# A fixed slot and engine for every operation of an attention and gated-projection kernel, in place of a greedy list order

## The chip, the core and the metric

One core of a Trainium2 chip runs the whole program. The metric is the device time of one execution in microseconds (us). The kernel before took 273.78 us, the median of 3 runs (273.67 to 274.02).

## What is computed

Four batches, 8 heads, 768 positions, head size 64, all in 32-bit floats. Attention sees a window of 96 past positions and the first 8 positions, with a linear bias per head; its output x goes through a 5-tap causal convolution that makes a gate, and through two 512 x 512 projections.

```python
scores = scale * np.matmul(q, k.transpose(0, 1, 3, 2))          # + bias, masked
a = np.exp(scores); a = a / (np.sum(a, axis=-1, keepdims=True) + 1e-09)
attn = np.matmul(a, v)                                          # x: (B, S, H * D)
gate = 1.0 / (1.0 + np.exp(-gate_pre))                          # gate_pre: 5 taps over x
return (gate * (x @ w_val) @ w_out).astype(np.float32)
```

## The kernel before, in words

The work is cut into 32 groups (`groups`: batch, half of the sequence, pair of heads), 3 steps of 128 queries each (96 steps), and 8 phases (a batch's half: 4 groups). The program is a list of 1,854 operations with names. Per group: `L` and `LV` load keys, queries and values (SP queue), `S` makes the score tiles on TensorE (PE). Per step: `AM` adds the bias and takes the row minimum (VectorE, DVE), `EX` takes the exponential (ScalarE, ACT), `RG` guards the sum (L511), `RC` inverts it (L514, DVE), `NM` multiplies the probabilities by it, once per head (L519), `PT` transposes them on PE through the identity (L530), `EV` copies the result out of PSUM. Per pair of groups `PV` multiplies with the values (L547, L553) into the PSUM tile x. From x come `XH` and `XL` (a rounded high part and the rest, for matmuls in the fp32r format), `HO` and `HI` (four columns of history, handed from half to half) and five `CV` (the taps, `gate`, L658 and L660). Per phase: `SG` (half a tanh), 16 `VM` (projection val, L706, three matmuls each), 4 `GM` (gate times val, L713), 4 `GH` and `GL` (high and low part, L720), 12 `OM` (projection o, L729, three matmuls each), 3 `OE` (evacuation, L740) and 3 `ST` (stores, L747).

The weights arrive as 64-bit floats and are decoded in the first part of the program: for each of 8 blocks `WL` (load, L404), `WA` (ACT), `W1` to `W4` (DVE), `WH` (high part), `WS` (sum on PE, L414 to L416), `WP` (its evacuation). `WARM` and `F` are matmuls on constants that fill PE's time at the start (L292); `plan.fill` puts such matmuls ahead of some transposes (L525).

Every operation has an urgency (constants such as `U_AM`, shifted per phase by `SHIFT`), a cost per engine that may run it, and what it depends on; `Plan.order` walks through time with a greedy rule: of the engine that is free first, the ready operation with the smallest urgency is taken, and an operation that several engines can run goes to the one that ends it first (with `SPARE` added). The order that comes out is each engine's instruction stream; instructions of one engine run in that order. `ring` makes an operation wait for the reader of a buffer that it will write again: the PSUM tiles of val and o share 2 banks (`moe`), the scores 2 per head, x 2.

```python
first = min(cands)
_, i, e = min(((ops[i][0], i, e) for t, i, e in cands if e == first[2] and t <= first[0] + LOOK[e]))
```

Of the kernel before, what the change touches and what calls it, by code (L numbers as in the profile page):

```python
# [16 lines left out]
WARM = 10  # L17
S_B, PT_B, X_B = 2, 2, 2
U_D1, RAW_B = -7.17, 4
FILL_UNTIL = 80.0  # L20
FILL_N, FILL_TO, U_F = 4, 1, -1.44
W_AT = (-0.71, 5.47, 7.21, 10.78, 17.96, 19.59, 23.37, 34.85)
W_PARTS = (2, 2, 2, 2, 2, 1, 1, 1)
WS_AT = (1, 4, 7, 10, 15, 19, 22, 24)
LOOK = {'vector': 0.0, 'scalar': 0.0, 'gpsimd': 0.0, 'tensor': 0.0, 'sync': 0.0}
SPARE = {'vector': 0.91, 'gpsimd': 0.02, 'scalar': -1.19}
XH_B, GATE_B, P_B, T_B, A_B, V_B, W_B, WT_B = 7, 2, 5, 8, 13, 6, 2, 1
U_XE, U_XH, U_CV, CV_STEP = -0.42, 0.63, 4.12, 0.63
U_AM, U_EX, U_RC, U_PT, U_EV, U_MOE = -0.95, -0.12, -5.71, -0.76, 4.31, 19.31
LAG = 2  # L30
JOIN = (0, 0, 0, 0, 1, 1, 1, 1, 1, 1, 1, 1, 1, 1, 1, 1)
U_L, U_LV, U_WL, U_S, U_HI, U_NM = -21.33, 0.02, -9.24, -2.77, 2.74, 0.27
U_PH = (-4.87, -0.47, -0.79, -0.74, -0.89, -0.15, -4.34, 2.72)
U_SG, U_GM, GM_STEP, U_GH, U_GL, U_O, VAL_T, O_T, U_OE = 13.64, -0.98, 0.8, -2.75, 0.05, 3.03, 5.41, 0.97, 1.65
SHIFT = {
# [49 lines left out]
class Plan:  # L85


    LAT = {'scalar': 0.2, 'vector': 0.19, 'gpsimd': 0.09, 'tensor': 0.24, 'sync': 0.05}
    DMA_LAT, DMA_RATE = 1.6, 330e3

    def __init__(self):
        self.ops, self.at, self.rings, self.then, self.fill = [], {}, {}, {}, {}

    def add(self, key, urgency, engines, fn, deps=(), nbytes=0, bank=None):

        assert key not in self.at, key
# [19 lines left out]
    def order(self, start):  # L116
        ops, at = self.ops, self.at
        n = len(ops)
        free, dma = dict(start), 0.0
        end, where = [0.0] * n, [""] * n  # L120
        left, users = [0] * n, [[] for _ in range(n)]
        deps = [sorted({at[d] for d in op[3]}) for op in ops]
        for i in range(n):
            left[i] = len(deps[i])
            for d in deps[i]:
                users[d].append(i)

        def ready(i, e):
            return max([end[d] + (0.05 if where[d] == e else self.LAT[where[d]]) for d in deps[i]], default=0.0)

        avail = [i for i in range(n) if not left[i]]
        out = []
        while avail:
            cands = []
            for i in avail:
                t = {e: max(free[e], ready(i, e)) for e in ops[i][1]}
                e = min(t, key=lambda x: t[x] + ops[i][1][x] + SPARE.get(x, 0.0))
                cands.append((t[e], i, e))
            first = min(cands)
            _, i, e = min(  # L140
                ((ops[i][0], i, e) for t, i, e in cands if e == first[2] and t <= first[0] + LOOK[e])
            )
            while i is not None:
                t = max(free[e], ready(i, e))
# [7 lines left out]
                if nbytes:  # L152
                    dma = max(dma, t + cost) + nbytes / self.DMA_RATE
                    end[i] = dma + self.DMA_LAT
# [893 lines left out]
```

## Time and profile before

| what | value |
|---|---|
| median of 3 runs | 273.78 us |
| the profiled execution: its own time | 274.04 us |
| its span, first to last instruction | 272.2 us |
| busy: PE, DVE, ACT, POOL | 260.0, 188.4, 209.4, 133.1 us |
| instructions | 8800 |
| chain that ended last, by engine | PE 76%, DVE 8%, DMA 6%, ACT 4% |

PE is TensorE (PEld its weight loads), POOL is GpSimd, SPq the queue that issues DMAs. A timeline row gives the start, the duration, the engine and line, the operation with output and inputs, and in brackets the idle time ahead of it and who ended it. Durations of neighbouring instructions of an engine overlap, so the price of one more in a dense run is the distance from start to start. A table of windows gives for each stretch the busy time of each engine.

### The profile page before, as it was taken

How to read it: one execution, taken by the hardware profiler on the slowest of the kernel's cores; microseconds unless marked ns; L12 is line 12 of the kernel's file. 1: busy time of each engine (PE TensorE's matmuls, PEld its weight loads, DVE VectorE, ACT ScalarE, POOL GpSimd, SP SyncE). 2: the span in 40 equal slices, each digit the busy share in tenths (PEclk: the TensorE clock that was granted, in tenths of full speed). 3: DMA queues.
4: the chain of work that ended last, by engine and by line, in shares of the span. 5: the costliest groups of instructions: out<-in, count | busy, mean ns of one | idle time of the engine just before them, and what ended most of it. 6: DMA issues, size and time to landing. Idle time of an engine off the chain costs nothing.

```text
span 272.2 us, 8800 instructions
## 1 busy us (share of the span) xinstructions
PE 260.0 (96%) x3125; PEld 216.7 (80%) x3127; DVE 188.4 (69%) x752; ACT 209.4 (77%) x701; POOL 133.1 (49%) x332
## 2 busy tenths in 40 slices
PE   8788999899899999999999999999999999999994
PEld 3447778677688888978898889888898889987983
DVE  4867999898939484785849493877769475494610
ACT  4899999888978788787778787987878695675322
POOL 5776666646346724364447634462447443350220
PEclk9999999999999999999999999999999999999998
DMA  5877876451645164513454153425551020002003
GB/s 169 300 256 220 318 258 236 138 164 56 209 118 191 47 192 141 158 67 95 172 169 135 56 207 119 159 69 161 166 177 51 4 79 39 2 39 81 0 5 122
DMA packets 16304, 36.37 MB, mean 134 GB/s; under 512 B 1920, under 2 KB 4480, under 8 KB 16256
## 3 DMA queue, kind: packets, MB, share of 16 engines
q1 hardware_dynamic: 16256, 35.75, 39.6%
q8 instruction: 27, 0.44, 0.7%
q14 instruction: 21, 0.17, 0.2%
HBM read 29.46 MB, written 6.29 MB: 131 GB/s over the span
## 4 chain that ended last, share of the span: by engine, by line
PE 76%; DVE 8%; DMA 6%; ACT 4%; issue 2%; SPq 2%; POOL 1%; POOLq 0%; ACTq 0%
PE o L729 25%; PE val L706 19%; PE pt L530 9%; PE s L486 9%; PE x L547 8%; DMA kq<-in_kq 6%; PE x L553 5%; DVE gate L658 4%; ACT p L504 2%; DVE xl L650 1%; DVE t L494 1%; PE wsum L414 1%; DVE g L713 1%; ACT gate L660 1%; POOL p L519 1%
## 5 line engine op out<-in xcount | busy, mean ns | idle before, releaser
L519 POOL TENSOR_SCALAR p<-p,rs 128x168 f32<-128x168 f32 (+1 forms) x186 | 79.9, 441 | 39.7 <-DVE rs L514 28.6
L504 ACT ACTIVATE p<-t,mins 128x168 f32<-128x168 f32 (+1 forms) x192 | 81.6, 427 | 7.9 <-DVE mins L494 5.8
L658 DVE SCALAR_TENSOR_TENSOR gate<-x,cwt,gate 128x384 f32<-128x384 f32 x128 | 78.3, 613 | 0.6
L494 DVE CUSTOM_DVE_ANT_0 t<-s,bias 128x168 f32<-128x168 f32 (+1 forms) x192 | 56.6, 318 | 7.6 <-PE s L486 7.5
L706 PE MATMUL val<-xh,wvh 128*128 128x384 f32 x128 | 48.1, 376 | 1.1 <-DVE g L713 1.1
L530 PE MATMUL pt<-ident,p 128*128 128x128 f32 x272 | 47.2, 278 | 1.4 <-ACT wvl L188 0.5
L188 ACT COPY a<-pt 128x384 f32<-128x384 f32 (+1 forms) x96 | 43.3, 454 | 6.6 <-PE pt L530 6.6
L511 POOL TENSOR_SCALAR sm<-sm 128x2 f32<-128x2 f32 x96 | 20.0, 208 | 54.2 <-ACT p L504 48.0
L720 POOL TENSOR_TENSOR gl<-g,gh 128x384 fp32r<-128x384 f32 x28 | 28.5, 1020 | 32.2 <-ACT gh L188 31.0
L729 PE MATMUL o<-woh,gh 128*128 128x512 f32 (+1 forms) x100 | 42.1, 421 | 1.7 <-DVE g L713 0.9
L706 PE MATMUL val<-xh,wvl 128*128 128x384 f32 x128 | 43.1, 337 | 0.0
L706 PE MATMUL val<-xl,wvh 128*128 128x384 f32 x128 | 43.1, 337 | 0.0
L530 PEld LDWEIGHTS pt<-ident,p 128*128 128x128 f32 x272 | 33.6, 140 | 10.5 <-POOL p L519 2.3
L729 PE MATMUL o<-wol,gh 128*128 128x512 f32 (+1 forms) x100 | 38.7, 387 | 0.0
L729 PE MATMUL o<-woh,gl 128*128 128x512 f32 (+1 forms) x100 | 38.6, 386 | 0.0
L504 ACT ACTIVATION_READ_ACCUMULATOR p<-t,mins 128x1 f32 x192 | 36.8, 192 | 0.0
L486 PEld LDWEIGHTS s<-kq 64*64 64x64 f32 x1088 | 30.3, 133 | 7.9 <-issue 4.4
L486 PE MATMUL s<-kq 64*64 64x104 f32 (+3 forms) x1088 | 34.3, 262 | 2.4 <-DMA kq<-in_kq 2.3
L514 DVE RECIPROCAL rs<-sm 128x2 f32<-128x2 f32 x96 | 15.5, 161 | 28.9 <-POOL sm L511 28.2
L650 DVE TENSOR_TENSOR xl<-x,xh 128x384 fp32r<-128x384 f32 x32 | 17.6, 554 | 22.0 <-ACT gate L660 12.6
L706 PEld LDWEIGHTS val<-xh,wvh 128*128 128x128 f32 x128 | 24.2, 189 | 3.7 <-DVE g L713 2.3
L188 ACT CAST xh<-x 128x384 fp32r<-128x384 f32 x32 | 15.2, 486 | 14.7 <-PE x L553 14.7
(154 smaller groups left out, 371.0 us busy)
## 6 DMA issues: line engine op xcount, KB each, us to landing
kq<-in_kq SPq DMA_DIRECT2D x16, 444.0 KB, 4.3
va<-in_va SPq DMA_DIRECT2D x16, 384.0 KB, 4.6
out<-ob SPq DMA_DIRECT2D x24, 256.0 KB, 2.1
kq<-in_kq SPq DMA_DIRECT2D x15, 392.0 KB, 3.9
va<-in_va SPq DMA_DIRECT2D x16, 320.0 KB, 3.9
w<-in_wv SPq DMA_DIRECT2D x8, 256.0 KB, 3.6
w<-in_wo SPq DMA_DIRECT2D x3, 512.0 KB, 4.4
w<-in_wo SPq DMA_DIRECT2D x2, 256.0 KB, 3.4
```

What stands on the lines that cost most here:

```text
L188: nc.scalar.copy(dst, src)
L486: nc.tensor.matmul(s[rows, u : u + w], T["rq", g][r, k * P + half * QH : k * P + (half + 1) * QH], T["rk", g][r, c : c + w], start=True, s ...
L494: nc.vector.tensor_tensor_reduce(out=t[:, :n], in0=T["s", s // HB, s % HB, j][:, :n], in1=bias[:, h, :P] if n == P else bias[:, h, P:], op ...
L504: nc.scalar.activation(T["p", s][:, j, :n], T["t", s, j][:, :n], AF.Exp, bias=mins[:, s, j : j + 1], scale=-1.0, accum_out=T["sm", s][:, j ...
L519: engine(e).tensor_scalar(out=pr, in0=pr, scalar1=rs, scalar2=1.0, op0=ALU.mult, op1=ALU.mult)
L530: nc.tensor.transpose(pt[:, i * P : (i + 1) * P], pr[:, c : c + P], ident)
L547: nc.tensor.matmul(T["x", g][rows(i), c0 : c0 + P], T["near", g][:, k, j], T["a", HB * g + k][:, j * P : (j + 1) * P], start=k == 0, stop= ...
L650: engine(e).tensor_sub(tile_of(("xl", g), [P, HT], F32R, "xl", XH_B), T["x", g][:, HIST:], T["xh", g])
L658: nc.vector.scalar_tensor_tensor(out=gt, in0=src, scalar=w, in1=gt, op0=ALU.mult, op1=ALU.add)
L706: nc.tensor.matmul(T["val", ph, m], (wvh, wvh, wvl)[r][:, m, c * P : (c + 1) * P], (T["xh", g], T["xl", g], T["xh", g])[r], start=(c == 0 ...
L720: engine(e).tensor_sub(tile_of(("gl", ph, m), [P, HT], F32R, "gl", 5), T["g", ph, m], T["gh", ph, m])
L729: nc.tensor.matmul(T[key][:, cols], (T["gh", ph, c], T["gl", ph, c], T["gh", ph, c])[r][:, rows], (woh, woh, wol)[r][:, c, cols], start=(c ...
```

## The change

`Plan.order` no longer simulates anything. Two tables replace urgencies, costs and rule: `SLOTS` gives each operation of a kind, in the order in which the kind's operations are added, a place in one list of 1,854, and `ENGINES` an engine where more than one can run it. `order` sorts by slot. `FILL` names the one transpose that still has a constant matmul ahead of it (before: 4 of them ahead of two transposes). Some dependencies are changed: the buffers `wh` and `wr` of the decoding are free again when `WS` has read them, not when `WP` has ended; `WH` waits for `W2` alone; `AM` names the bias of the head that it really uses; `F` waits for the scores alone. `PV` depends on `HI` (the history's write into x) as before. Arithmetic and shapes stay.

```diff
+SLOTS = {
+    "L": (
+        2, 5, 8, 16, 89, 132, 136, 183, 188, 275, 391, 400, 503, 506, 601, 606, 618, 655, 719, 760, 829, 853, 943,
...
+ENGINES = {
+    "BIAS": "SSSSSGSGSGGSGSSS",
...
+    "GL": "GGVVGVVGGGGGGGVVGVVVVGGGGVGGGVVG",
+    "OE": "SSSSSSSSVSSVSSVSSSVSVSVVS",
 }
+FILL = {7: 1}
...
+        kind = key[0]
+        n = self.count[kind] = self.count.get(kind, -1) + 1
+        e = NAMES[ENGINES[kind][n]] if kind in ENGINES else engines[0]
...
+    def order(self):
+        for slot, _, _, deps in self.ops:
+            assert all(self.ops[self.at[d]][0] < slot for d in deps), "an operation is listed before one that it needs"
+        return [(fn, e) for _, e, fn, _ in sorted(self.ops, key=lambda op: op[0])]
...
-        for _ in range(plan.fill.get(plan.at["PT", s], 0)):
+        for _ in range(FILL.get(s, 0)):
...
-                deps += plan.ring("wh", WT_B, key, [("WP", i), ("WH", i)])
+                deps += plan.ring("wh", WT_B, key, [("WS", i), ("WH", i)])
...
-                deps += plan.ring("wr", WT_B, key, [("WP", i)])
+                deps += plan.ring("wr", WT_B, key, [("WS", i)])
...
-        plan.add(("WH", i), u + 0.5, {ACT: 0.52, DVE: 0.335}, lambda e, i=i: w_high(e, i), [("W2", i), ("W3", i)])
+        plan.add(("WH", i), (ACT, DVE), lambda e, i=i: w_high(e, i), [("W2", i)])
...
-                         [("S", g), ("BIAS", 2 * groups[g][2] + j, int(full))] + plan.ring("t", T_B, key, [("EX", s, j)]))
+                plan.add(key, (DVE,), lambda e, s=s, j=j: add_bias(s, j),
+                         [("S", g), ("BIAS", 2 * groups[g][2] + head_at(groups[g][2], j), int(full))]
+                         + plan.ring("t", T_B, key, [("EX", s, j)]))
```

What moves between engines, counted in the two orders: to DVE go 53 of POOL's 186 `NM`, 51 of its 96 `RG` and 9 of its 28 `GL`; from ACT, DVE takes 9 first taps of `CV`, 7 `GH`, 7 `OE` (one of them a half), 6 `EV`, 5 `XH`, 7 copies of history and one `WH`; ACT takes 3 `BIAS` from POOL.

The SP queue at the start of the program issues the first DMAs (kq: keys and queries of a group, va: values, w: a weight block, craw: the taps). Before:

```order
L225 DMA counts_i<-in_counts 128x4
L266 DMA kq_118<-in_kq 128x2x128
L266 DMA kq_118<-in_kq 128x2x272
L404 DMA w_123<-in_wv 128x2x256 x2
L443 DMA craw<-in_cw 128x40
L273 DMA va_135<-in_va 128x640
L259 DMA kq_144<-in_kq 128x784
```

and with the change:

```order
L331 DMA counts_i<-in_counts 128x4
L372 DMA kq_118<-in_kq 128x2x128
L372 DMA kq_118<-in_kq 128x2x272
L504 DMA w_121<-in_wv 128x2x256 x2
L365 DMA kq_124<-in_kq 128x784
L365 DMA kq_131<-in_kq 128x784
L504 DMA w_133<-in_wv 128x2x256 x2
L541 DMA craw<-in_cw 128x40
L365 DMA kq_147<-in_kq 128x784
L379 DMA va_169<-in_va 128x640
```

The keys of the second group now stand ahead of the taps and of the first values, and those of the third and fourth group follow before any values.

DVE after the scores of the first group, in the decoding (the numbers behind a name are those of buffers and steps). Before:

```order
L514 RECIPROCAL rs_0_222<-sm_0_183 128x2
L384 TENSOR_SCALAR ('w', 0)_y_195<-('w', 0)_h_213 128x512
L457 TENSOR_SCALAR cw_y_215<-cw_y_215 128x20
L458 SCALAR_TENSOR_TENSOR cw_h_250<-craw_83,cw_y_215 128x20
L459 TENSOR_SCALAR cw_y_215<-cw_h_250 128x20
```

and with the change:

```order
L609 TENSOR_SCALAR sm_0_190<-sm_0_190 128x2
L612 RECIPROCAL rs_0_205<-sm_0_190 128x2
L617 TENSOR_SCALAR p_0_189<-p_0_189,rs_0_205 128x128
L480 TENSOR_SCALAR ('w', 0)_y_202<-('w', 0)_y_202 128x512
L617 TENSOR_SCALAR p_0_189<-p_0_189,rs_0_205 128x128
L483 SCALAR_TENSOR_TENSOR ('w', 0)_h_235<-w_0_121,('w', 0)_y_202 128x512
```

Guard, reciprocal and both norms of the first step now stand on DVE one behind the other, where the guard and the norms were on POOL.

PE in the third phase, around the first matmul of its fourth val tile (val_2_3), which takes the PSUM bank that `GM` of val_2_1 frees. Before, from the last matmul into val_2_1:

```order
L706 MATMUL val_2_1_2065<-xh_11_1894,wvl_80 128x384
L706 MATMUL val_2_2_2213<-xh_9_1596,wvh_79 128x384
L706 MATMUL val_2_2_2213<-xl_9_1614,wvh_79 128x384
L706 MATMUL val_2_2_2213<-xh_9_1596,wvl_80 128x384
L706 MATMUL val_2_2_2213<-xh_10_1891,wvh_79 128x384
L706 MATMUL val_2_2_2213<-xl_10_1896,wvh_79 128x384
L706 MATMUL val_2_2_2213<-xh_10_1891,wvl_80 128x384
L706 MATMUL val_2_3_2250<-xh_8_1593,wvh_79 128x384
```

and with the change:

```order
L766 MATMUL val_2_1_2254<-xh_11_1998,wvl_80 128x384
L628 MATMUL pt_45_2298<-ident_71,p_45_2080 128x128 x3
L766 MATMUL val_2_2_2309<-xh_8_1647,wvh_79 128x384
L766 MATMUL val_2_2_2309<-xl_8_1673,wvh_79 128x384
L766 MATMUL val_2_2_2309<-xh_8_1647,wvl_80 128x384
L628 MATMUL pt_46_2318<-ident_71,p_46_2112 128x128 x3
L766 MATMUL val_2_2_2309<-xh_9_1665,wvh_79 128x384
L766 MATMUL val_2_2_2309<-xl_9_1742,wvh_79 128x384
L766 MATMUL val_2_2_2309<-xh_9_1665,wvl_80 128x384
L628 MATMUL pt_47_2333<-ident_71,p_47_2115 128x128 x3
L766 MATMUL val_2_3_2341<-xh_8_1647,wvh_79 128x384
```

Three transposes now lie between the two, beside six matmuls of val.

## Rows read from the trace of the kernel before

**Rows 1.** The page, part 1: busy us, share of the span, instructions, by engine.

```profile
PE 260.0 (96%) x3125; PEld 216.7 (80%) x3127; DVE 188.4 (69%) x752; ACT 209.4 (77%) x701; POOL 133.1 (49%) x332
```

**Rows 2.** Windows: stretch, us, busy PE, PEld, DVE, ACT, POOL, clock, DMA share, GB/s.

```profile
10.00:20.00 10.00, 8.39 (x92) 5.12 (x97) 7.34 (x40) 8.87 (x34) 7.52 (x18) 1.00 0.79 270
20.00:30.00 10.00, 9.30 (x155) 7.88 (x155) 8.19 (x36) 9.87 (x38) 6.73 (x17) 1.00 0.84 253
30.00:40.00 10.00, 8.86 (x151) 6.63 (x150) 9.32 (x36) 9.38 (x34) 6.29 (x16) 1.00 0.81 289
40.00:50.00 10.00, 9.10 (x80) 7.79 (x80) 9.82 (x34) 9.13 (x29) 6.29 (x13) 1.00 0.59 206
50.00:60.00 10.00, 10.00 (x138) 7.46 (x136) 8.60 (x33) 9.13 (x30) 5.40 (x12) 1.00 0.42 135
...
140.00:170.00 30.00, 30.00 (x419) 26.32 (x414) 20.78 (x88) 24.27 (x86) 15.45 (x41) 1.00 0.41 132
```

**Rows 3.** PE's timeline: the second group's scores, and waits further on.

```profile
10.53 1.16 PE L486 MATMUL s<-kq 64*64 64x128 f32 x32 [1.58 <-DMA kq<-in_kq]
...
71.22 0.50 PE L729 MATMUL o<-woh,gh 128*128 128x512 f32 x1 [0.84 <-ACT ob L740]
...
78.04 1.20 PE L547 MATMUL x<-a,va 128*64 128x128 f32 x18
...
115.57 0.34 PE L706 MATMUL val<-xh,wvl 128*128 128x384 f32 x1
116.42 0.45 PE L706 MATMUL val<-xh,wvh 128*128 128x384 f32 x1 [0.51 <-DVE g L713]
```

**Rows 4.** Timelines of the SP queue and of ACT: the second group's keys, what follows.

```profile
3.72 0.48 SPq L443 DMA_DIRECT2D craw<-in_cw  x1
4.23 0.43 SPq L273 DMA_DIRECT2D va<-in_va  x1
4.71 0.43 SPq L259 DMA_DIRECT2D kq<-in_kq  x1
...
12.09 0.37 ACT L188 COPY a<-pt 128x256 f32<-128x256 f32 x1 [1.14 <-PE pt L530]
```

**Rows 5.** Groups by form: line, engine, operation, count, busy us, mean ns, idle before.

```profile
L519 POOL TENSOR_SCALAR p<-p,rs 128x168 f32<-128x168 f32 x154 | 67.6, 451 | 31.6 <-DVE rs L514 22.1 <-DVE x L642 2.4 <-PE o L729 1.8
L511 POOL TENSOR_SCALAR sm<-sm 128x2 f32<-128x2 f32 x96 | 20.0, 208 | 54.2 <-ACT p L504 48.0 <-ACT x L188 0.5
L720 POOL TENSOR_TENSOR gl<-g,gh 128x384 fp32r<-128x384 f32 x28 | 28.5, 1020 | 32.2 <-ACT gh L188 31.0
L658 DVE SCALAR_TENSOR_TENSOR gate<-x,cwt,gate 128x384 f32<-128x384 f32 x128 | 78.3, 613 | 0.6
L740 ACT ACTIVATE ob<-o 128x512 f32<-128x512 f32 x23 | 13.5, 588 | 4.2 <-PE o L729 4.1
```

**Rows 6.** Timelines of DVE and POOL: two norms on DVE, and POOL beside the second.

```profile
153.82 0.31 DVE L519 TENSOR_SCALAR p<-p,rs 128x168 f32<-128x168 f32 x1
...
184.45 1.00 DVE L519 TENSOR_SCALAR p<-p,rs 128x168 f32<-128x168 f32 x1
...
184.34 1.00 POOL L720 TENSOR_TENSOR gl<-g,gh 128x384 fp32r<-128x384 f32 x1
```

**Rows 7.** PE's timeline: a transpose, val behind it, and scores behind val.

```profile
141.78 0.49 PE L530 MATMUL pt<-ident,p 128*128 128x128 f32 x3
142.02 0.42 PE L706 MATMUL val<-xh,wvh 128*128 128x384 f32 x1
142.28 0.33 PE L706 MATMUL val<-xl,wvh 128*128 128x384 f32 x1
142.45 0.34 PE L706 MATMUL val<-xh,wvl 128*128 128x384 f32 x1
...
146.82 0.34 PE L706 MATMUL val<-xh,wvl 128*128 128x384 f32 x1
147.08 1.11 PE L486 MATMUL s<-kq 64*64 64x168 f32 x36
```

More of the change, by code (lines that the diff above doesn't have):

```diff
@@ L27 @@
[L27 to L34, printed above, removed]
@@ L114, in ring @@
         return deps
[L116 to L144, printed above, removed]
-                cost, nbytes = ops[i][1][e], ops[i][4]
-                if ops[i][5] is not None and t < FILL_UNTIL:
-                    bank = max([end[at[d]] + self.LAT[where[at[d]]] for d in ops[i][5]], default=0.0)
-                    self.fill[i] = max(0, min(12, int((t - max(free[e], bank) - 0.15) / 0.215)))
-                avail.remove(i)
-                where[i], free[e] = e, t + cost
-                end[i] = t + cost
-                if nbytes:
-                    dma = max(dma, t + cost) + nbytes / self.DMA_RATE
-                    end[i] = dma + self.DMA_LAT
-                out.append((t, len(out), i, e))
-                for u in users[i]:
-                    left[u] -= 1
-                    if not left[u]:
-                        avail.append(u)
-                i = self.then.get(i)
-        assert len(out) == n, "operations wait for each other"
-        return [(ops[i][2], e) for _, _, i, e in sorted(out)]
@@ L362, in attention_moe @@
     for h in range(H):
-        for part, cost in enumerate(({DVE: 0.2, POOL: 0.33, ACT: 0.3}, {DVE: 0.25, POOL: 0.4, ACT: 0.33})):
-            plan.add(("BIAS", h, part), 3 * (h // 2) + part - 1 + 0.1 * (h % 2), cost,
-                     lambda e, h=h, part=part: biases(e, h, part), [("DIST", part)])
+        for part in range(2):
+            plan.add(("BIAS", h, part), (DVE, POOL, ACT), lambda e, h=h, part=part: biases(e, h, part),
+                     [("DIST", part)])
     def f64_abs(raw, n, nm):
@@ L461, in taps2 @@
         ve.tensor_add(cwt.rearrange("p a b -> p (a b)"), h.bitcast(F32), r)
-    plan.add(("CWL",), 0, {SP: 0.5}, load_taps, (), P * NC * TAPS * 8)
-    plan.add(("CWA",), 3, {ACT: 0.15}, taps, [("CWL",)])
-    plan.add(("CW",), 4, {DVE: 0.6}, taps2, [("CWA",)])
+    plan.add(("CWL",), (SP,), load_taps)
+    plan.add(("CWA",), (ACT,), taps, [("CWL",)])
+    plan.add(("CW",), (DVE,), taps2, [("CWA",)])
     def scores(g):
@@ L546, in pv @@
             for g, j, i in runs:
-                nc.tensor.matmul(T["x", g][rows(i), c0 : c0 + P], T["near", g][:, k, j], T["a", HB * g + k][:, j * P : (j + 1) * P],
-                                 start=k == 0, stop=False)
+                nc.tensor.matmul(T["x", g][rows(i), c0 : c0 + P], T["near", g][:, k, j],
+                                 T["a", HB * g + k][:, j * P : (j + 1) * P], start=k == 0, stop=False)
         for k in range(1 - hf, HB):
@@ L633, in attention_moe @@
             key = ("EV", s)
-            plan.add(key, s + U_EV, {ACT: 0.36 if full else 0.255, DVE: 0.463 if full else 0.335},
-                     lambda e, s=s: evac_pt(e, s), [("PT", s)] + plan.ring("a", A_B, key, [("PV", g)]))
+            plan.add(key, (ACT, DVE), lambda e, s=s: evac_pt(e, s), [("PT", s)] + plan.ring("a", A_B, key, [("PV", g)]))
     def hist_in(e, g):
@@ L691, in attention_moe @@
                 deps.append(("CV", g - 1, 0))
-            plan.add(key, u + U_CV + CV_STEP * k, {DVE: 0.53} if k else {DVE: 0.53, ACT: 0.48},
-                     lambda e, g=g, k=k: conv(e, g, k), deps)
+            plan.add(key, (DVE,) if k else (DVE, ACT), lambda e, g=g, k=k: conv(e, g, k), deps)
     def half_tanh(g):
@@ L821, in decide @@
         ve.tensor_copy(flag, f)
-    plan.add(("FA",), NSTEP + 3, {DVE: 0.3}, row_mins, [("AM", s, j) for s in range(NSTEP) for j in range(2)])
-    plan.add(("FB",), NSTEP + 3, {PE: 0.06}, row_mins_t, [("FA",)] + plan.ring("pt", PT_B, ("FB",), [("FC",)]))
-    plan.add(("FC",), NSTEP + 4, {DVE: 0.7}, decide, [("FB",)])
+    plan.add(("FA",), (DVE,), row_mins, [("AM", s, j) for s in range(NSTEP) for j in range(2)])
+    plan.add(("FB",), (PE,), row_mins_t, [("FA",)] + plan.ring("pt", PT_B, ("FB",), [("FC",)]))
+    plan.add(("FC",), (DVE,), decide, [("FB",)])
     with tc.manual_schedule():
-        for fn, e in plan.order({SP: 1.6, PE: 0.6, ACT: 1.9, DVE: 2.6, POOL: 0.5}):
+        for fn, e in plan.order():
             fn(e)
```

256 lines of the change are left out of this document (143 added, 113 removed), and 106 rows, old and new, of tables (SHIFT, SLOTS).

## The prediction

> **What bounds the kernel now.** Read the page's first part before anything else [rows 1]: PE is busy for 96% of the span and no other engine for more than 77%. The durations of matmuls overlap there, so the next view is the table of windows [rows 2], which separates two kernels in one. From 50 us on PE is busy without a gap (30.00 of 30 us in the stretch from 140 to 170), at the full granted clock of 1.00, while ACT has 24.27 us of work in these 30, DVE 20.78 and POOL 15.45. There the order on the other engines is worth nothing until it makes PE wait. In the first 60 us it is another matter: the weights are decoded beside the attention, ACT is busy for 8.87, 9.87, 9.38, 9.13 and 9.13 of each 10 us, DVE for 7.34 rising to 9.82, and PE has gaps. This stretch is held by ACT, with DVE close behind.
>
> The third view is PE's timeline, for what its gaps wait on [rows 3]. The largest is at the start: the scores of the second group come only at 10.53 us, released by their DMA; ahead of their 1.58 us of waiting PE ran matmuls on constants. Later waits are few: 0.84 us at 71.22, on an evacuation by ACT, and 0.85 us from start to start at 115.57 where the next val matmul is usually 0.17 later [rows 3, 7], so 0.7 lost, on the gating by DVE. A wait like the second returns once, one period (60 us) later. In sum the steady part loses 0.8 + 0.7 + 0.7 = 2.2 us to waits that can be seen. What the change can win is bounded by these and by what the start gives back.
>
> **The start.** The keys of the second group are issued at 4.71 us, behind the taps (0.48 us to the next issue) and the first values (0.43), and free PE at 10.53 [rows 3, 4]. The new order moves both behind the keys. That is 0.91 us of issuing, and 340 KB (20 and 320) less ahead of them; at the 270 GB/s of the stretch from 10 to 20 us [rows 2] 340 KB are 1.26 us. So the scores can start between 0.9 and 2.2 us earlier. PE's gain there counts only if ACT, which bounds the stretch, is fed earlier: its one large wait is 1.14 us, ending at 12.09 with the first transpose's copy [rows 4]. I take 1.1 us; bounds 0 and 2.2. Moving taps and values back is costed at nothing: the taps are wanted by the first convolution, behind the first P.V, and the values by that P.V. If their cover is gone, P.V waits for values that now stand behind three loads of keys and a weight block more; that is inside the upper bound of zero gain.
>
> For the rest of the decoding I sum ACT's idle time between 20 and 60 us: 0.13 + 0.62 + 0.87 + 0.87 = 2.49 [rows 2]. Up to the fifth P.V the two orders give PE the same work within two `VM` and one transpose, and ACT has issued 8 instructions fewer (4 `SG`, and one each of `GH`, `OE`, `WH`, `HI`) and 4 more (3 `BIAS`, one `EX`): four fewer net, at up to 0.59 us each [rows 5] 2.4 us of relief. DVE takes the guards and norms that stood on POOL, and DVE is as full as ACT there, so I do not believe in all of it: 1.2 us, half of the idle time; bounds 0 and 2.5. The looser waits of the decoding (`wh` and `wr` free after `WS`, `WH` after `W2`) shorten chains that ACT and DVE work through one instruction after the other; they are part of this term and carry none of their own.
>
> **The steady part.** At the wait of 116 us the order shows what changes: from the last matmul of val_2_1 to the first of val_2_3, which needs the gating of val_2_1, stood six matmuls, 6 x 0.17 = 1.04 us. Now three transposes of 0.24 [rows 7] lie there too, 1.8 us or more. The 0.7 us are covered, if DVE comes to the gating in time. I count 1.6 of the 2.2 us as won, bounds 0 and 2.2, since a list order that waited in three places will not wait in none.
>
> Against it stands a cost on PE itself. A val matmul behind a transpose takes 0.26 us to the next start where later ones take 0.17, and scores behind val start 0.26 after it instead of 0.17 [rows 7]: 0.09 for each change between fp32r and fp32. Counted in the two orders, changes into val or o are 88 before and 87 now, but changes from val or o into scores or P.V rise from 16 to 25. Nine more at 0.09 cost 0.8 us; bounds 0 and 1.
>
> **DVE's new load.** This is where the change could turn against itself. DVE takes 53 norms, 51 guards, 9 `GL`, 9 first taps, and some 25 instructions of the kind of an evacuation (7 `GH`, 7 `OE`, 6 `EV`, 5 `XH`). A norm takes 0.31 us where POOL is nearly free, and 1.00 where POOL is in a `GL` that started before it and ends at 185.34 [rows 6]. No guard on DVE is in the trace; POOL's guard takes 0.208, a longer price than its two columns should need, and I take it. At the low price of a norm: 53 x 0.31 = 16.4; 51 x 0.208 = 10.6; 18 x 0.613 = 11.0 for `GL` and taps, which have the same 384 columns; 25 x 0.588 = 14.7 [rows 5, 6]; 52.7 us in all, some 6.6 per stretch of 30 us. DVE then has 20.8 + 6.6 = 27.4 us of work in 30 [rows 2], with 2.6 us of cover. POOL loses 53 x 0.451 + 51 x 0.208 + 9 x 1.02 = 43.7 us, 5.5 per stretch, and is left with 10 of 30. Of the 7.4 norms that DVE then has per stretch a third, 2.4, should meet POOL at work, for half of an instruction of 0.45 to 1.02 us: about 0.9 us, inside the cover. I charge 0.6 us over the kernel for DVE being late in a few places; bounds 0 and what the rival below costs.
>
> The two rows on DVE's norms are what the Trainium skill would expect: SBUF — State Buffer, "Who interferes with whom", says that VectorE in a two-port mode (copies, casts, tensor_scalar between SBUF tiles) and GpSimd take one port pair in turn, for a whole instruction. By that rule the 51 guards on DVE would wait as well, which no row here shows: 51 times a third times half a norm's 0.45 is an estimate of 3.8 us more on DVE, 0.5 per stretch. By it DVE's charge in the sum would be 1.1 us in place of 0.6.
>
> **The sum.** The end is unchanged: 45 matmuls of val and 48 of o follow the last P.V in both orders; the one transpose of the decision moves in among these o, 0.1 us. The fillers of L525 lay in waits. So -1.1 - 1.2 - 1.6 + 0.8 + 0.6 + 0.1 = -2.4 us against the profiled execution's 274.04, or 271.6; the median lies 0.26 below that execution, which makes **271.4 us**. The likeliest case alone reaches from 269.5 to 273.2.
>
> **Rivals.** *DVE becomes the bound (slower).* Place: the phases, where norms and `GL` alternate. Price: 0.69 us per norm that meets a `GL`. From 4 meetings per stretch (4 x 0.69 = 2.8 against 2.6 of cover) every further one delays gating and row minima, and PE behind them. At 5 of 7.4 the overrun is 0.85 us per stretch, over 7 stretches 6; with the gain of the start left (2.3), the switching (0.8) and the steady waits not won, that is 273.8 + 6 + 0.8 - 2.3 = 278. For it: DVE runs its instructions in the order written, so a late norm holds up the gating and the minima behind it, and DVE would be at 91% of a stretch. Against it: POOL has a third less to do and meets less, and 0.9 us of delay per stretch is within the cover. The two rows of a norm, 0.31 and 1.00, lie far apart, so a chance of 0.18.
>
> *The start is held by ACT and DVE whatever the order.* Both are near 9.5 of 10 us there [rows 2], and the gain at 10.53 is eaten by what follows. Then -1.6 + 1.5 is left: 273.7, no change that can be told (0.2%, 0.55 us, is about what a measurement of this kernel can tell). Chance 0.16.
>
> *The start gives everything back.* Keys 2.2 us earlier, ACT without a pause (2.5), all steady waits gone (2.2), DVE never late: -6.9 + 0.9 = -6.0, so 267.8. For it: a chain of guard, reciprocal and norms on one engine saves the hand-overs, of which POOL's guards and norms show 54.2 and 31.6 us of idle time ahead [rows 5]. Against it: this idle time lies on no chain of PE's in the steady part. Chance 0.20.
>
> **The numbers.** Forecast 0.46, full gain 0.20, together 0.66 faster; held start 0.16, same; 0.18 slower. The range from 266.5 to 275.5 takes in the forecast's bounds, the held start and most of the full gain, and leaves out the larger part of the slower rival.
>
> **What would show it.** Right: the scores of the second group start between 8.3 and 9.6 us; ACT's busy share between 10 and 60 us is no lower than before at the same progress; no wait near 116 and 176 us; DVE at about 240 us busy, its norms mostly near 0.31, their mean below 0.5. Wrong: norms of 0.7 and more on DVE, PE waiting for gating or row minima in the phases after 80 us (the slower rival); or the fifth P.V still at 78.04 us [rows 3] (the held start). If the fifth P.V comes by 74, the full gain is the case.

## The result, and the profile after

The changed kernel takes 271.22 us, the median of 4 runs (270.85 to 271.48); the kernel before took 273.9 beside it (4 runs, 273.67 to 274.83). The ratio is 0.9895, with a 95% interval from 0.9868 to 0.9921. The forecast was 271.4 us. The profiled execution has a span of 269.0 us where the one before had 272.2, so 3.2 us are to be found.

The page's first part of the changed kernel, as in [rows 1]:

```profile
PE 256.5 (95%) x3124; PEld 215.8 (80%) x3124; DVE 220.2 (82%) x907; ACT 191.2 (71%) x662; POOL 85.8 (32%) x216
```

POOL lost 47 us, DVE gained 32, ACT lost 18. DVE stays 20 us below the 240 that the prediction summed up: the durations of its instructions rose by 46.7 us in sum (the prediction had 52.7), but they overlap, and its busy time rose by 31.8 only. The windows of [rows 2], now:

```profile
10.00:20.00 10.00, 8.95 (x104) 5.85 (x97) 9.30 (x56) 9.61 (x37) 4.03 (x11) 1.00 0.81 283
20.00:30.00 10.00, 8.43 (x148) 6.16 (x147) 10.00 (x45) 10.00 (x38) 3.87 (x9) 1.00 0.81 274
30.00:40.00 10.00, 9.93 (x134) 8.57 (x132) 9.71 (x48) 9.63 (x34) 3.93 (x11) 1.00 0.77 278
40.00:50.00 10.00, 9.88 (x170) 8.15 (x171) 9.42 (x34) 10.00 (x35) 5.11 (x13) 1.00 0.34 111
...
140.00:170.00 30.00, 30.00 (x390) 26.28 (x389) 25.41 (x105) 22.37 (x81) 8.46 (x22) 1.00 0.37 122
```

The columns are PE, PEld, DVE, ACT, POOL, granted clock, DMA share and GB/s. ACT and DVE are full or nearly so through the decoding; PE, which had gaps there, is at 9.9 of 10 from 30 us on. In the stretch from 140 us DVE has 25.41 of 30, not 27.4.

PE's timeline at the two places of [rows 3] that moved most, the scores of the second group and the fifth P.V, and its last matmul:

```profile
9.03 1.17 PE L584 MATMUL s<-kq 64*64 64x128 f32 x32 [1.83 <-DMA kq<-in_kq]
...
74.36 1.53 PE L645 MATMUL x<-a,va 128*64 128x128 f32 x24
...
262.10 0.28 PE L789 MATMUL o<-wol,gh 128*128 128x256 f32 x1
```

The scores start at 9.03 in place of 10.53, the fifth P.V at 74.36 in place of 78.04. PE's last matmul ends at 262.38; before, the last one started at 268.04 and ended at 268.31. **PE is done 5.9 us earlier, and the program only 3.2.** So 2.7 us were lost behind PE's last matmul: the span ends 3.9 us behind it before, 6.6 us now. What stands there now shows in DVE's timeline, and in the waits of SP's queue from 258 us on. (SPq is the queue, a q behind an engine its sequencer; the numbers are us in total, times, and the longest. L888 is the branch on the flag, L1099 the program's last barrier; in the kernel before they are L833 and L1044.)

```profile
260.89 0.42 DVE L803 TENSOR_SCALAR ob<-o 128x256 f32<-128x256 f32 x1 [0.72 <-PE o L789]
261.23 0.27 DVE L870 TENSOR_REDUCE far<-rmt 1x1 f32<-1x128 f32 x1
...
262.31 0.14 DVE L876 CAST flag<-slow 1x1 int32<-1x1 f32 x1
```

```profile
SPq L1099 <- DVEq L888: 1.7, 1, 1.7
...
SPq L1099 <- PEq L888: 0.9, 1, 0.9
```

In the kernel before the flag was written at 251.00, 17 us ahead of PE's end, and SP waited there for a store's evacuation and for PE's side of the barrier, hardly for PE's branch and not for DVE's:

```profile
SPq L747 <- ACTq L833: 2.5, 1, 2.5
SPq L1044 <- PEq L1044: 0.9, 2, 0.8
...
SPq L1044 <- PEq L833: 0.2, 1, 0.2
```

The flag decides whether the general path runs (`tc.If`). Every engine loads it behind its last instruction and branches on it. The new list puts its transpose (`FB`) and its making (`FC`) among the last of the 1,854 operations.

### The profile page after: what moved, and what is told of

It is laid out like the page before. It is cut to its first block, busy times and chain, and to the rows that moved or that the text cites. A ratio compares the mean times of both kernels' runs of the same rounds, so it can differ in the third digit from the quotient of the medians.

```text
span 269.0 us, 8650 instructions
## 1 busy us (share of the span) xinstructions
PE 256.5 (95%) x3124; PEld 215.8 (80%) x3124; DVE 220.2 (82%) x907; ACT 191.2 (71%) x662; POOL 85.8 (32%) x216
## 4 chain that ended last, share of the span: by engine, by line
PE 78%; ACT 9%; DVE 4%; issue 1%; POOL 1%; ACTq 0%; DVEq 0%
PE o L789 24%; PE val L766 23%; PE pt L628 10%; PE s L584 8%; PE x L645 8%; PE x L651 4%; ACT p L602 3%; DVE gate L724 1%; ACT a L294 1%; DVE t L592 1%; ACT gate L726 1%; PE wsum L514 1%; POOL p L617 1%; ACT woh L294 1%; ACT gate L759 0%
## 5 line engine op out<-in xcount | busy, mean ns | idle before, releaser
L724 DVE SCALAR_TENSOR_TENSOR gate<-x,cwt,gate 128x384 f32<-128x384 f32 x128 | 77.2, 611 | 4.8 <-ACT gate L726 3.1
L617 POOL TENSOR_SCALAR p<-p,rs 128x168 f32<-128x168 f32 (+1 forms) x133 | 54.2, 419 | 77.0 <-DVE rs L612 62.5
L592 DVE CUSTOM_DVE_ANT_0 t<-s,bias 128x168 f32<-128x168 f32 (+1 forms) x192 | 56.9, 318 | 10.1 <-PE s L584 9.6
L294 ACT COPY a<-pt 128x384 f32<-128x384 f32 (+1 forms) x90 | 40.6, 458 | 16.4 <-PE pt L628 16.3
L766 PE MATMUL val<-xh,wvh 128*128 128x384 f32 x128 | 47.0, 367 | 0.0
L602 ACT ACTIVATION_READ_ACCUMULATOR p<-t,mins 128x1 f32 x192 | 37.8, 197 | 0.0
L780 POOL TENSOR_TENSOR gl<-g,gh 128x384 fp32r<-128x384 f32 x19 | 19.2, 1014 | 29.4 <-ACT gh L294 26.1
L609 POOL TENSOR_SCALAR sm<-sm 128x2 f32<-128x2 f32 x45 | 8.7, 193 | 61.3 <-ACT p L602 57.1
L645 PE MATMUL x<-a,va 128*64 128x128 f32 x384 | 24.7, 277 | 0.0
L766 PEld LDWEIGHTS val<-xl,wvh 128*128 128x128 f32 x128 | 24.2, 189 | 0.0
L766 PEld LDWEIGHTS val<-xh,wvl 128*128 128x128 f32 x128 | 24.0, 188 | 0.0
```

Of the source, the lines that this page charges most:

```text
L294: nc.scalar.copy(dst, src)
L592: nc.vector.tensor_tensor_reduce(out=t[:, :n], in0=T["s", s // HB, s % HB, j][:, :n], in1=bias[:, h, :P] if n == P else bias[:, h, P:], op ...
L602: nc.scalar.activation(T["p", s][:, j, :n], T["t", s, j][:, :n], AF.Exp, bias=mins[:, s, j : j + 1], scale=-1.0, accum_out=T["sm", s][:, j ...
L617: engine(e).tensor_scalar(out=pr, in0=pr, scalar1=rs, scalar2=1.0, op0=ALU.mult, op1=ALU.mult)
L645: nc.tensor.matmul(T["x", g][rows(i), c0 : c0 + P], T["near", g][:, k, j], T["a", HB * g + k][:, j * P : (j + 1) * P], start=k == 0, stop= ...
L724: nc.vector.scalar_tensor_tensor(out=gt, in0=src, scalar=w, in1=gt, op0=ALU.mult, op1=ALU.add)
```

## The experiments

Theory: the order of the list won nearly 6 us on PE, and the late flag gave some 2.5 of them back. Rivals: the end is longer because of the stores; the gain comes from the loads, or from the new engines, and not from the order.

### 1 and 2. The flag early in the changed kernel, late in the one before

```diff
-    "FA": (1814,),   "FB": (1845,),     "FC": (1849,),
+    "FA": (1715.5,), "FB": (1781.5,),   "FC": (1785.5,),
```

> The changed kernel with the decision moved to where the kernel before has it: the maximum over the row minima right behind the last row minimum, its transpose ahead of the last P.V, the flag behind it, some 20 us ahead of the end in place of 0.6 us. Theory (the late flag lengthens the end): the changed kernel's span ends 6.18 us after its last store is issued, that of the kernel before 3.45; so 2.7 us come off the 271.2, to 268.5 (267.9 to 269.2), and the last store stays within 0.4 us of 262.8. Rival A (the end is longer because of the stores: three within 2.6 us, two of them behind DVE's evacuations, median landing 3.2 us where it was 2.1): no change, 270.9 to 271.5. Rival B (only SP's own load of the flag, 0.5 us of waiting behind the last store, counts): 270.4 to 270.8.

```diff
-    plan.add(("FB",), ..., [("FA",)] + ...)
+    plan.add(("FB",), ..., [("FA",), ("OM", NPH - 1, HB - 1, NC - 1, 0)] + ...)
```

> The kernel before with the transpose of the decision, and so the flag, held back until the first half of the last o tile is done, 0.7 us ahead of PE's last matmul. The mirror image of the first experiment. Theory (the late flag lengthens the end): 2.7 us more than the kernel before, 276.6 (275.9 to 277.2), all of it behind the last store. Rival A (stores and evacuations, which are untouched here): no change, 273.6 to 274.2. Rival B (SP's own load alone): 274.3 to 274.7.

Measured: 269.53 us with the early flag (0.9839, 0.9823 to 0.9854), 276.31 with the late one (1.0091, 1.0077 to 1.0105, against 273.86). From PE's last matmul to the span's end it is 4.3 us with the early flag (263.59 to 267.9) and 6.2 with the late one (268.34 to 274.5), against 6.6 and 3.9 in the two kernels themselves. Taking the flag away from the end wins 2.3 us of it, putting it there costs 2.3: the theory, at a little less than its 2.7. (The time of the first, 269.53, lies outside its 267.9 to 269.2 all the same; see below.) Stores and evacuations are the same in each pair, so rival A falls, and rival B's half microsecond is too small. In the late kernel SP's queue shows the line that the kernel before did not have:

```profile
SPq L1044 <- DVEq L833: 1.1, 1, 1.1
SPq L1044 <- PEq L1044: 0.9, 2, 0.8
SPq L1044 <- PEq L833: 0.8, 1, 0.8
```

The wait that ends last is the one for PE's branch. The rows of the branch's line, in the changed kernel (a row gives the duration in ns, and the start; PEld's sequencer is PE's, and DVE's EVENT_SEMAPHORE is its next instruction behind the branch):

```profile
L888 PEldq COMPARE_BRANCH  x1: 4809/4809/4809, 263.1 to 263.1; - x1
L888 DVEq COMPARE_BRANCH  x1: 72/72/72, 263.1 to 263.1; - x1
...
L888 DVEq EVENT_SEMAPHORE  x1: 21/21/21, 267.1 to 267.1; - x1
```

and PE's in the kernel before, the first, the second and the twelfth experiment:

```profile
L833 PEldq COMPARE_BRANCH  x1: 3697/3697/3697, 266.9 to 266.9; - x1
```

```profile
L888 PEldq COMPARE_BRANCH  x1: 4592/4592/4592, 262.3 to 262.3; - x1
```

```profile
L833 PEldq COMPARE_BRANCH  x1: 3594/3594/3594, 269.6 to 269.6; - x1
```

```profile
L888 PEldq COMPARE_BRANCH  x1: 4682/4682/4682, 260.9 to 260.9; - x1
```

Counted in us from the end of PE's last matmul:

| kernel | PE's branch starts | takes | ends | span ends |
|---|---|---|---|---|
| before | −1.4 | 3.7 | 2.3 | 3.9 |
| before, flag late (experiment 2) | 1.2 | 3.6 | 4.8 | 6.2 |
| changed | 0.7 | 4.8 | 5.5 | 6.6 |
| changed, flag early (experiment 1) | −1.3 | 4.6 | 3.3 | 4.3 |
| changed, flag hidden (experiment 12) | −1.5 | 4.7 | 3.2 | 4.2 |
| changed, engines of before (experiment 6) | 0.5 | 3.9 | 4.4 | 5.4 |

In each of them the span ends 1.0 to 1.6 us behind PE's branch. With the flag written in time PE loads it and branches while its last matmuls still run; with a late flag the branch begins 2.0 to 2.7 us later, and the end with it. The load itself is short (0.49 us on PE). DVE's branch holds DVE for 3.9 us in the changed kernel, but it is over before PE's. Why PE's takes 3.6 to 4.9 us, and longer in most of the changed kernels than in the one before, no run shows.

The first kernel's time fell by 1.7 only, because something else was lost: in its profile PE ends 1.2 us later than in the change. Half of that is the second group's scores, which start at 9.60 in place of 9.03. The other half are the last 45 val matmuls; from the start of the first to the first o behind them they go from 246.48 to 255.02 us, 8.54 where the change has 7.92 (245.76 to 253.68) and the kernel before 8.40 (251.32 to 259.72). In DVE's timeline of the first experiment the decision stands ahead of the taps and the gating that these val tiles wait for:

```profile
245.64 0.27 DVE L870 TENSOR_REDUCE far<-rmt 1x1 f32<-1x128 f32 x1
...
246.72 0.14 DVE L876 CAST flag<-slow 1x1 int32<-1x1 f32 x1
246.79 0.60 DVE L728 TENSOR_SCALAR gate<-x,cwt 128x384 f32<-128x384 f32 x1
```

So the late place had a sense for PE: 0.6 us of val, bought with 2.3 us of end. Experiment 8 keeps both.

### 3. The first loads as they were

```diff
-    "CWL": (11,),   "LV": (20, 22, ...)
+    "CWL": (4.2,),  "LV": (4.4, 22, ...)
```

> The changed kernel with two DMAs put back where they stood: the taps and the first values are issued ahead of the second group's keys. Theory of the prediction (keys earlier are worth 1.1 us, bounds 0 and 2.2): scores of the second group from 9.03 us to between 10.1 and 11.2, the fifth P.V from 74.4 to 75.5, the time from 271.2 to 272.3. Rival (ACT and DVE hold the start, each at 9.3 to 10.0 of 10 us): the scores move as much, the fifth P.V stays below 74.8, the time below 271.6.

Measured: 273.38 us, the median of 12 runs from 271.08 to 275.06; ratio 0.9978 (0.9951 to 1.0006). The scores of the second group start at 9.71, only 0.68 later, but those of the third at 14.84 in place of 12.58, the first P.V is 2.27 us later (22.42) and PE ends 2.37 later. What happens between the two scores is TensorE's clock. PE's timeline of this experiment, and its window from 11 to 14 us:

```profile
5.58 0.82 PE L584 MATMUL s<-kq 64*64 64x168 f32 x24 [0.59 <-DMA kq<-in_kq]
6.33 1.04 PE L396 MATMUL warm<-const-bfloat16-1.0 128*128 128x512 bf16 x4
9.71 1.18 PE L584 MATMUL s<-kq 64*64 64x128 f32 x32 [2.33 <-DMA kq<-in_kq]
10.83 0.69 PE L628 MATMUL pt<-ident,p 128*128 128x128 f32 x2
11.31 3.28 PE L396 MATMUL warm<-const-bfloat16-1.0 128*128 128x512 bf16 x8
```

```profile
11.00:14.00 3.00, 3.00 (x9) 1.28 (x10) 3.00 (x19) 2.53 (x10) 0.88 (x2) 0.50 0.64 248
```

After waits of 0.59 and 2.33 us PE's granted clock is 0.50 from 11 to 14 us, the lower of its two levels (1.2 GHz), and the eight fillers on constants that the list puts there take 3.28 us. In the profile of the change they take 1.91, at 1.00:

```profile
10.41 1.91 PE L396 MATMUL warm<-const-bfloat16-1.0 128*128 128x512 bf16 x8
```

The 12 runs fall in line with the mean clock that each lists: the three at 271.08 to 271.87 have 0.993 to 0.997, the nine at 273.05 to 275.06 have 0.980 to 0.992. By itself that mean is no proof, since it takes in the end of the span: the change's profiled execution lists 0.991 at 270.85 us, with 1.00 through the start and 0.61 from 263 us on. The change has such executions too (experiment 11), so the old loads make them frequent and do not alone cause them. So the loads' order is worth little by itself (under 1 us, which single profiles can hardly tell: the nine profiles of kernels with the new list and its first loads have the second scores anywhere from 8.51 to 9.86), and some 2 us or more where the wait costs the clock. The rival falls (fifth P.V at 76.65). Of the theory the direction is left: it had the scores at 10.1 or later, the fifth P.V at 75.5 and the time at 272.3, and the time lost is twice its 1.1 us, by another mechanism.

### 4, 6 and 7. The engines

In the fourth kernel the guards and norms of steps 0 to 26 go to POOL, in the sixth all 178 operations that changed engines go back to those of the kernel before (59 norms had gone to DVE and 6 from it, 12 `GL` to it and 3 from it: the counts given with the change are net), in the seventh every norm from step 27 on goes to DVE.

```diff
         e = NAMES[ENGINES[kind][n]] if kind in ENGINES else engines[0]
+        if kind in ("RG", "NM") and 0 <= key[1] < 27: e = "gpsimd"      # fourth
+        if kind == "NM" and key[1] >= 27: e = "vector"                  # seventh
```

> The changed kernel with every guard and norm of the first 27 steps on POOL: 15 guards and 8 norms leave DVE, the order in the list stays. Theory (guard, reciprocal and norm one behind the other on DVE save hand-overs, and that is what the start won beyond the predicted 2.3 us): the fifth P.V comes 1 to 2 us later than 74.4, the time is 272 to 273. Rival (DVE is the fuller engine of the start, and 15 x 0.18 + 8 x 0.30 = 5.1 us of work less on it help): the fifth P.V comes at 74.4 or earlier, the time is 270 to 271.3.

> The changed kernel's places in the list with the engines of the kernel before: 178 operations go back, 65 norms, 51 guards and 15 GL among them. Theory A (the order makes the gain, the engines hardly any, as the guards and norms of the first 27 steps on POOL did not matter): 270.5 to 272, the fifth P.V at 74 to 75. Theory B (the engines make it: what the start won beyond the loads, about 2 us, and the steady waits, about 2, come back): the fifth P.V at 76 or later, the time 273 to 276, with waits of PE on POOL's norms or DVE's gating after 80 us.

> The changed kernel with the other 87 norms of steps 27 to 95 on DVE too: the suspected cost doubled. At 0.30 us a norm that is 26 us more, DVE at some 246 of 269, 29 to 30 of 30 us in a stretch. The rival of the prediction (norms meet POOL's instructions and wait 0.69 us each, DVE becomes the bound): the mean of a norm on DVE is 0.5 or more, 276 to 282 us, with PE waiting for DVE in every phase. Theory from the trace after the change (norms beside POOL take 0.30 all the same): their mean stays below 0.35, PE waits only where DVE is full, 271 to 273.5.

Measured: 270.4 us (0.9889, 0.9865 to 0.9913), 270.79 (0.9885, 0.987 to 0.9899) and 276.68 (1.0108, 1.0085 to 1.0131).

The fourth kernel lies 0.17 to 0.18 us ahead of the change at every P.V from the second to the last, with second keys that landed 0.5 us earlier: neither the hand-overs nor DVE's relief show. The sixth has its fifth P.V at 74.26, 0.1 us earlier than the change, although POOL has its 128 us of work again and DVE only 187:

```profile
PE 257.6 (96%) x3124; PEld 216.0 (80%) x3124; DVE 186.7 (69%) x752; ACT 205.6 (76%) x701; POOL 128.0 (48%) x332
```

It falls back mostly between 150 and 165 us (the P.V at 164.03 comes at 164.76), and PE ends 1.0 us later than in the change. Its time does not differ, since its end is 5.4 us and not 6.6: PE's branch starts 0.2 us earlier there and takes 3.87 us in place of 4.81. Theory A holds: **the gain is the list's**. Of the 5.9 us at PE's end the moves between engines carry about 1.0, and nothing of the 3.7 at the fifth P.V. What the places, the looser dependencies and the fillers that went each carry, no run took apart.

The seventh shows the price of the prediction's slower rival. DVE's norms in it, grouped by form, and its windows from 80 us on:

```profile
L619 DVE TENSOR_SCALAR p<-p,rs 128x168 f32<-128x168 f32 x121 | 36.1, 316 | 0.4
...
L619 DVE TENSOR_SCALAR p<-p,rs 128x128 f32<-128x128 f32 x25 | 7.8, 324 | 0.0
```

```profile
80.00:110.00 30.00, 29.47 (x345) 24.47 (x347) 27.88 (x123) 22.85 (x81) 3.04 (x8) 1.00 0.47 153
...
140.00:170.00 30.00, 28.68 (x306) 24.46 (x306) 28.06 (x117) 20.88 (x76) 3.18 (x8) 1.00 0.42 139
```

The mean norm takes 0.32 us, as the second theory had it, so the norms do not stand and wait for POOL. All the same the kernel is 5.5 us slower than the change: at 28 of 30 us DVE is late for PE, which is no longer at 30. Neither expectation was right in full: the time is the rival's, the mechanism is plain load. Five norms did wait, each of them started beside a `GL` on POOL (0.64 to 1.07 us); one of them on DVE's timeline, and POOL's:

```profile
143.55 1.07 DVE L619 TENSOR_SCALAR p<-p,rs 128x128 f32<-128x128 f32 x1
```

```profile
143.54 1.00 POOL L782 TENSOR_TENSOR gl<-g,gh 128x384 fp32r<-128x384 f32 x1 [2.33 <-ACT gh L296]
```

### 5 and 9. The new loads in the old list

In the fifth kernel, the list before issues the keys of the second and third group and the second weight block ahead of the taps and of the first two blocks of values; in the ninth only the second group's keys go ahead of the first values. All other streams stay.

```diff
+        want = [at[k] for k in (("L", 1), ("L", 2), ("WL", 1), ("CWL",), ("LV", 0), ("LV", 1))]   # fifth
+        want = [at[k] for k in (("CWL",), ("L", 1), ("LV", 0))]                                    # ninth
```

> The kernel before with nothing but its first DMAs in the changed order: keys of the second and third group and the second weight block ahead of the taps and the first values. Theory (the order of the loads is worth some 2.2 us of the gain, what the opposite exchange cost the changed kernel): the first P.V comes at 19.4 to 20.5 us in place of 21.55, PE's end moves as much, the time is 271.7 to 272.8. Rival (the list before is held by ACT and DVE in the decoding, so that an earlier start is eaten up): the first P.V comes earlier, the fifth stays within 0.5 us of 78.0, the time is 273.4 to 274.2.

> The kernel before with one exchange at SP: the second group's keys ahead of the first values, behind the taps; all else stays. (The larger exchange in the fifth experiment put the taps late, for which ACT of the kernel before waits early.) Theory (the loads' order is worth its time in this list too, as long as nothing waits for what is moved back): the scores of the second group come 0.4 to 1.5 us earlier than 10.5, the first P.V 0.3 to 1.3 earlier than 21.55, PE ends as much earlier, the time is 272.6 to 273.6. Rival (ACT and DVE hold the decoding of the old list): the scores come earlier, the first P.V and the time stay within 0.3 us (273.6 to 274.2).

Measured: 277.47 us (1.0136, 1.0119 to 1.0154) and 273.7 (0.9996, 0.9984 to 1.0008). The theory falls in both, and in the fifth the rival too (fifth P.V at 81.11); in the ninth the rival has the time, though neither the scores nor the first P.V (22.09). In the fifth kernel the scores of the second group do start at 9.20, but ACT of the old list decodes the taps early, and stands still for them:

```profile
11.89 0.22 ACT L456 ACTIVATE cw_y<-craw 128x20 f32<-128x20 f32 x1 [2.26 <-DMA craw<-in_cw]
```

The exponentials of the first group are queued behind it; PE waits 2.98 us for its next probabilities, its granted clock falls (0.57 from 14 to 17 us), and the third group's scores come at 18.01 instead of 14.04. In the ninth the keys were issued 0.49 us earlier (4.22) and landed no earlier (scores at 10.73, before 10.53), in a profile of the slowest of its 12 executions (274.54). In these two tries the loads' order won nothing without the list that uses it.

### 8, 10, 11 and 12. A flag that is early and in nobody's way

```diff
-    "FA": (1814,),   "FB": (1845,),    "FC": (1849,),    "OE": "...SVSVVS"
+    "FA": (1715.5,), "FB": (1829.5,),  "FC": (1830.5,),  "OE": "...SVSSSS"
```

The transpose lies behind the first six of the last o matmuls, the flag behind the last gating, and the last two evacuations that stood on DVE go to ACT. The tenth kernel also loads the flag on every engine between the halves of the last o tile. The eleventh is the change once more, the twelfth the eighth, on one chip.

> The changed kernel with the decision early but out of DVE's way: the maximum behind the last row minimum, the transpose among the first matmuls of the last o tiles, the flag behind the last gating, some 6 us ahead of the end; the last two evacuations that stood on DVE go to ACT. In the first experiment the last 45 val matmuls took 8.54 us where the change has 7.92, with the decision's seven DVE instructions (1.2 us) ahead of the gating. Theory (those 0.6 us were DVE's, and the end needs the flag only a few us ahead): val in 7.9 to 8.0, the span ends 3.8 to 4.4 us behind PE's last matmul, 268.4 to 269.1. Rival (val was late for another reason, or a flag 6 us ahead is still too late): 269.3 us or more.

> The eighth kernel (decision hidden) with the flag's load moved on every engine from behind the last instruction into the list, between the two halves of the last o tile. Theory (what the end still spends behind PE's last matmul, 4.1 us, holds a load of the flag on PE and ACT, about 0.5 us, and a load amid the matmuls costs PE less than that): 268.3 to 268.8. Rival A (the store's landing and the branch fill that time, so the load is hidden already): 268.9 to 269.3. Rival B (the load stops PE by more than it saves): 269.4 to 270.5.

> The changed kernel once more, beside the next one on one chip, so that the two can be compared directly. 271.2 us (270.8 to 271.6), the span ending 6.0 to 6.6 us behind PE's last matmul.

> The eighth kernel again, the best so far. Theory (a late flag is worth 2.3 us of end, and the hidden place costs DVE and PE nothing): 2.0 to 2.6 us less than the changed kernel beside it, 268.6 to 269.2. Rival (the 269.1 was a better chip or earlier keys): less than 1.5 us between the two.

Measured: 269.08 us (0.9827, 0.9807 to 0.9848), 268.94 (0.9844, 0.9806 to 0.9883), and side by side 270.85 for the change (0.987, 0.9855 to 0.9885) and **268.47** for the hidden flag (0.9794, 0.9781 to 0.9808), against 274.13 for the kernel before. The last 45 val matmuls of the eighth take 7.99 us, and its span ends 4.1 us behind PE. In the twelfth the flag is written at 257.16, PE ends at 262.35 and the span at 266.6, 4.25 later; the wait for DVE's branch is gone from SP's queue:

```profile
SPq L1099 <- PEq L888: 1.2, 1, 1.2
SPq L1099 <- PEq L1099: 0.6, 2, 0.5
```

So 2.4 us less than the change beside it: the theory (its time, 268.47, lies 0.1 below the range given). Loading the flag inside the list does nothing that can be told from this (4.4 us of end): rival A of that run, by its time just so. PE's branch ends 2.2 us behind its last matmul there, a microsecond earlier than in the twelfth, and SP then waits for the stores to land. The hidden flag beats the kernel before by 2.1% and the change by 0.9%.

The eleventh run's profile, of its slowest execution (272.93 us; the other four 270.47 to 270.98), shows a fall of the clock without any edit. The same stretch as in experiment 3, of the changed kernel itself:

```profile
9.54 1.41 PE L584 MATMUL s<-kq 64*64 64x128 f32 x32 [2.44 <-DMA kq<-in_kq]
...
11.78 2.63 PE L396 MATMUL warm<-const-bfloat16-1.0 128*128 128x512 bf16 x7 [0.22 <-issue]
```

The keys came half a microsecond later than in the first profile, the granted clock from 11 to 14 us was 0.55, so at its lower level for most of them, and the first P.V came at 22.25 in place of 20.15: 2.1 us, which it keeps to the end.

## Why the prediction was right, and where it was not

The number was right (271.4 for 271.22) and its sum was not: two errors of about 3 us each, of opposite sign, lay in it. That they cancel to 0.2 us is luck.

**The start: −1.1 and −1.2.** The scores of the second group at 9.03 lie in the 8.3 to 9.6 given, and ACT's share did not fall. To the fifth P.V the change won 3.7 us, where the terms had 2.3 and the wait at 71.22 us [rows 3], which is gone, some 0.6 more. That the fifth P.V comes by 74 was named as the mark of the full gain, and it nearly does. The work ahead of that P.V is about even: the new order has 32 matmuls of scores more there, which the prediction did not count, and 6 of val fewer. The mechanism of the first term was too simple: 340 KB less ahead of the keys are 0.7 us at the scores in one pair of profiles (experiment 3), less than the same loads scatter by, and the rest is a risk, the clock at its lower level after some of these waits. The second term halved ACT's idle time because DVE would be as full; both engines are now full (10.00 of 10 from 20 to 30 us), and experiments 4 and 6 say that the relief of ACT and the guards on DVE have no part in it. What remains, some 2 us of decoding, is the list's; which piece of it (places, dependencies, fillers) was not tried.

**The steady waits: −1.6.** They are gone as forecast, at 116 and at 176. From the fifth P.V to its last matmul PE takes 188.0 us where it took 190.3, so 2.2 less, where the prediction's terms for this part add up to a loss of a few tenths. One wait I had not seen: the last 45 val matmuls, 8.40 us before and 7.92 after. In the changed kernel the decision on DVE can bring it back (experiment 1). In the kernel before it was not the decision: with that moved to the end (experiment 2) they take 8.74 us. There DVE's `XL` starts, as before, when ACT's tap ends: at 252.47 after 1.44 us of waiting, and in the kernel before at 252.49 after 0.16:

```profile
252.47 0.56 DVE L650 TENSOR_TENSOR xl<-x,xh 128x384 fp32r<-128x384 f32 x1 [1.44 <-ACT gate L660]
```

With the list's places and the engines of the kernel before they take 7.91 (experiment 6), so this half microsecond is the list's too. The rest of the difference I cannot give to rows.

**Switching: +0.8.** The price of one change stands. PE's timeline of the changed kernel in its third phase:

```profile
101.70 0.34 PE L766 MATMUL val<-xh,wvl 128*128 128x384 f32 x1
101.88 0.49 PE L628 MATMUL pt<-ident,p 128*128 128x128 f32 x3
102.12 0.42 PE L766 MATMUL val<-xh,wvh 128*128 128x384 f32 x1
102.38 0.34 PE L766 MATMUL val<-xl,wvh 128*128 128x384 f32 x1
...
103.98 0.40 PE L789 MATMUL o<-woh,gl 128*128 128x512 f32 x1
104.22 0.39 PE L789 MATMUL o<-wol,gh 128*128 128x512 f32 x1
104.53 1.02 PE L584 MATMUL s<-kq 64*64 64x128 f32 x32
```

Val behind a transpose takes 0.26 to the next start, and o takes 0.31 instead of 0.24 when scores follow; a transpose behind val costs nothing more than val's usual 0.18, so it was right to count only the changes into scores and P.V. No run took this term by itself.

**DVE late: +0.6, and the rival at 278.** DVE's norms after the change:

```profile
L617 DVE TENSOR_SCALAR p<-p,rs 128x168 f32<-128x168 f32 x48 | 13.8, 301 | 0.3
...
L609 DVE TENSOR_SCALAR sm<-sm 128x2 f32<-128x2 f32 x51 | 8.6, 177 | 2.7 <-ACT p L602 2.5
```

The forecast mean below 0.5 is 0.30, and PE's matmuls never wait for gating or minima. What was mis-sized is DVE's load: the 27.4 us of 30 sum durations that overlap, and it is 25.4. The step that failed here is "a third, 2.4, should meet POOL at work": of the 59 norms three start beside POOL, each beside a norm there, and take 0.31 to 0.34; none starts beside a `GL`. I took meetings as chance, and the fixed list leaves none of the dear ones. One guard does meet a `GL` (0.74 us in place of 0.18). By the rule of the Trainium skill in SBUF — State Buffer, "Who interferes with whom", which by the prediction's estimate puts DVE's charge at 1.1, such a guard waits too. That one agrees; beside POOL's norms the rows are mixed: the three norms show no wait, two of five guards do (0.33 and 0.24 us), and in experiment 6 one norm takes 0.53. The rival's place was right all the same, as experiment 7 shows: at 28 of 30 us DVE costs 5.5 us, but by load, and the change stops at 25.4.

**"The end is unchanged": +0.1.** This is the step that failed most. I priced the decision's transpose on PE at 0.1 us and took DVE's part and the flag's readers for nothing. The order showed that transpose moving in among the last o matmuls, so it was to be seen that the flag would be written about at PE's end (262.31 us, PE ends at 262.38). Asked who waits for it, the answer is every engine, and it costs 2.3 us (experiments 1 and 2), 2.7 between the two profiles: PE's branch starts 2.14 us later against PE's last matmul, takes 1.11 longer, and what follows it is 0.58 shorter. The Trainium skill has it that a taken branch out of the window that is already fetched waits for its code by DMA (Runtime: NRT & Kernel Launch, "Instruction fetch mechanics"). No run here shows whether that is what PE's branch waits for, though the instruction queues (q8 and q14) move seven packets from 262 us to the end of the changed kernel's span.

In spans: −3.7 to the fifth P.V, −2.2 from there to PE's end, +2.7 behind it, together −3.2.

## What to carry to other kernels

Read the end of a program as a stage of its own: PE's last matmul, then the last store, then whatever every engine must still read. A value that all engines branch on belongs some microseconds ahead of the end, behind the last work that the bounding engine waits for, so that a slow branch runs beside the last work. When an order is changed, ask of each moved operation who waits for it, also where it costs its own engine nothing. And a sum that comes out right is not yet shown right: its terms want their own marks in the trace, and here the mark of PE's end would have shown both errors at once.

## What was not expected of the hardware

- The same branch has very different prices. On PE it took 3.6 to 4.9 us in the 14 profiles, and on DVE 2.8 to 3.9 us passed from it to the next instruction; on ACT, POOL and SP these were 0.1 to 0.5.
- A wait at the start has two prices. In two executions of the changed kernel the second scores started at 9.03 and at 9.54 us; the second time the granted clock from 11 to 14 us was 0.55 and the half microsecond became 2.1. The eighth kernel waited 2.37 us for the same keys and kept 1.00 throughout, so one wait's length does not decide it alone.
- A norm on DVE (128 x 128) that starts as a `GL` starts on POOL takes 1.07 us in place of 0.30, and ends just behind it. One of the changed kernel that starts at 67.14 us amid four of POOL's norms takes 0.31, one of experiment 6 at 156.41 us, just ahead of a norm on POOL, 0.53.
- Keys issued 0.49 us earlier landed no earlier in the one profile of experiment 9; what such landings scatter by is larger (scores at 8.51 to 9.86 us with the same first loads).
